# Step 1 of a fused convolution and gated-MLP kernel: other homes for six convolution taps, and four additions on another engine

## The chip, the cores and the metric

One core of a Trainium2 chip runs the whole program. The metric is the device time of one execution in microseconds (us), the median of several runs. The engines are TensorE (PE in the profile, with its weight loads PEld), VectorE (DVE), ScalarE (ACT), GpSimd (POOL) and SyncE (SP). SP and POOL also issue DMAs; a DMA that adds to its destination (an accumulation) is issued by POOL here.

## The reference, cut to what matters

```python
# x (8, 4096, 192), weight (8, 7): a causal depthwise convolution over the sequence, softmaxed taps per head
w = softmax(weight, axis=-1)
x_pad = np.concatenate([np.zeros((B, 6, D)), x], axis=1)
x_unf = x_pad[:, idx, :].reshape(B, S, K, H, group)      # idx: 7 shifted windows
x = np.einsum('hk,bskhg->bshg', w, x_unf).reshape(B * S, D)
# w_in (192, 2048), w_out (2048, 192)
h = x @ w_in
g = h * (1.0 / (1.0 + np.exp(-1.702 * h)))
return (g @ w_out).astype(np.float32)
```

## The kernel before

The 32768 tokens are worked in 32 steps ("big" in the code), each of 2 x 512 tokens. A step has a first half (`hidden`), which computes `x @ w_in` in fp32 by a scheme of fewer products over sums of operands, and the gelu, and a second half (`second`), which computes `g @ w_out` and stores. Step 0 has its own code. Each engine runs its instructions in the order in which the code issues them; the framework adds a wait on a semaphore where an instruction needs what another engine or a DMA has written, and also where it overwrites what another still has to read.

The order inside `hidden` is written out in the list `HIDDEN`. Its entries: `mm` is a product of TensorE (line 709) into one of four pairs of PSUM banks p0 to p3; `copy` and `join` move and combine banks (ScalarE or VectorE, lines 802, 804 and 817); `gelu i` is ScalarE's activation into rows of the buffer `g` (line 826 from PSUM in two halves, line 833 from SBUF in one instruction); `early` is a sum of rows of `g` on VectorE (lines 435 and 437); `over` makes the common sum of the next step (pair 12) by two additions and sends it across partitions with two DMAs of SP (line 609); `ve` makes further sums of the next step on GpSimd; `fetch` is the first product of the next step, which reads pair 12.

While step s runs, the convolution of a later step is made, in three blocks (0, 1, 2) of two column groups. A tap k of a block is one ScalarE instruction that multiplies the shifted input by the tap's weight, into a place of its own, its home (tap 0 goes to its final place in `conv_t`, "own"). The seven homes are then added in a tree: accumulation (i, j) adds home j to home i, in the order (1,2), (3,4), (5,6), (0,1), (3,5), (0,3). Homes are free places in larger buffers: `spot(i)` is one of the two pieces of `osbs` (0, 1), of three pieces of `room` (2 to 4), or, from 5 on, a block of `g`, and a home is a half of a spot (first index 0 or 2 of four).

Step 1 is special, because it makes step 2's convolution late. Blocks 0 and 2 of step 2 are tapped by ScalarE earlier (line 570) and added by DMA accumulations of GpSimd (line 600). The middle block, block 1, is tapped from the list `beside`: after the second `join` of step 1, each further join runs one entry, and entries 0 to 6 hold two weight sums of VectorE and tap j of the middle block (`middle_tap`, ScalarE, line 1096). Homes 1 to 6 are in the table `MIDDLE` as (spot, half), and `middle_tree` issues the block's accumulations (line 1108). The last two accumulations of block 2, (3,5) and (0,3), are left over in the list `tree` and issued by `end_taps` inside `middle_tap`, at tap 3 and tap 5, so they stand between the middle block's accumulations in GpSimd's queue; four accumulations for sums of w_out (line 482, "forms") stand ahead. `over` of step 1 runs at the third `turn`.

The rows of `g` that a spot covers are written by certain gelus. For the homes of this case: spots 11 and 12 at half 0 by gelu 5, spots 11 and 12 at half 2 by gelu 7, spot 14 at half 0 by gelu 8, spot 15 at half 0 by gelu 9, spot 17 at half 2 by gelu 14. The gelus stand in `HIDDEN` in the order 0, 6, 4, 1, 2, 5, 9, 3, 10, 11, 8, 7, 14, 12, 15, 13. Spot 14 at half 0 and spot 17 at half 2 hold pairs 17 and 18 of step 1, which early products of step 1 read.

Of the kernel before, what the change touches and what calls it, by code (L numbers as in the profile page):

```python
# [15 lines left out]
def kernel(  # L16
# [64 lines left out]
    vec, act = nc.vector, nc.scalar  # L81
# [56 lines left out]
    def spot(i):  # L138

        if i >= SPOTS:  # L140
            return block(*divmod(i - SPOTS, NG))
        flat = osbs[:, i * BLK : (i + 1) * BLK] if i < 2 else room[:, ROOMS[i - 2], :]
        return flat.rearrange("p (k t) -> p k t", k=NG)
# [47 lines left out]
    def pair(big, b):  # L191

        if b in SPOT_V:
            s, k = SPOT_V[b]
            return spot(s)[:, k : k + 2, :]
        o, x = places_of(big, b)
        return conv_t[:, o : x + 1 : x - o, :]

    def own(big):
        return conv_t[:, big % 2 * NR : big % 2 * NR + NR, :]  # L200
# [156 lines left out]
    for c in range(NC):  # L357
        part = sel[:, c, :].rearrange("i (h q) -> i h q", h=2)
        for sign in (1, -1):
            nc.gpsimd.affine_select(  # L360
                out=part,
# [71 lines left out]
    def add_up(v, dst, a, op, b, eng=vec):  # L433
        if op == "+":
            eng.tensor_add(v(dst), v(a), v(b))  # L435
        elif op == "-":
            eng.tensor_sub(v(dst), v(a), v(b))  # L437
        elif op == "n":
            vec.scalar_tensor_tensor(
                out=v(dst), in0=v(a), scalar=-1.0, in1=v(b), op0=ALU.mult, op1=ALU.subtract  # L440
            )
        else:
            vec.tensor_scalar_mul(v(dst), v(a), -1.0)
# [99 lines left out]
    def conv_src(big, c, k, ns=slice(0, 2)):  # L543
        return xts[big][:, c, ns, Q - PAD + k : Q - PAD + k + T]
# [43 lines left out]
    tree, to_add = [], {}  # L588
# [8 lines left out]
    def end_taps(left=0):  # L597
        while len(tree) > left:
            out, src = tree.pop(0)
            nc.gpsimd.dma_start(out=out, in_=src, accum_op=ALU.add)  # L600

    def sum_of(big, item, eng=None):

        add_up(lambda i: pair(big, i)[:, 0, :], *item, eng=eng or nc.gpsimd)
# [8 lines left out]
    def cross_run(big, b0, b1, eng=None):  # L613

        (o, x), n = places_of(big, b0), b1 - b0
        cross(conv_t[:, x : x + n, :], conv_t[:, o : o + n, :], eng)
# [158 lines left out]
    def hidden(big, tiles, work):  # L775
# [102 lines left out]

        def over():
            for item in SUMS_F:  # L880
                sum_of(big + 1, item)
            cross_run(big + 1, *FIRST)

        def when_more(f):
# [27 lines left out]
        def add(eng, what):  # L912
# [4 lines left out]
        do = dict(  # L917
            add=add, mm=mm, copy=copy, join=join, gelu=gelu, turn=turn, tap=tap, early=early, vl=vl, fetch=lambda: fetch(big + 1, tiles[NEXT[0]]) if more else None,
            over=when_more(over), ve=when_more(lambda i: sum_of(big + 1, SUMS_H[i])),
            vc=when_more(lambda b: cross_run(big + 1, b, b + 1)),  # L920
        )
# [7 lines left out]
    def second_first(between, fetch, last_taps):  # L929
# [152 lines left out]
        for j in range(max(K, (n - 2) // 2)):  # L1082
            def more(j=j):
                sums_w_in(FETCH[0], 3 + 2 * j, 5 + 2 * j)
                if j < K:
                    middle_tap(j)
            beside.append(more)

    after_copy, beside = [], []
    MIDDLE = ((11, 0), (12, 0), (3, 0), (15, 0), (11, 2), (3, 2))  # L1090

    def middle_tap(k):
        dst = own(2)[:, 2:4, :]
        s, h = MIDDLE[k - 1]
        home = spot(s)[:, h : h + 2, :] if k else dst
        act.mul(home, conv_src(2, 1, k), cw[:, 1, k : k + 1])
        end_taps({3: 1, 5: 0}.get(k, 2))
        middle_tree({2: 1, 4: 1, 6: 2}.get(k, 0))

    middle_pairs = [(1, 2), (3, 4), (5, 6), (0, 1), (3, 5), (0, 3)]  # L1100
# [1 line left out]
    def middle_tree(n):  # L1102
        for i, j in [middle_pairs.pop(0) for _ in range(n)]:
            out, src = (
                spot(MIDDLE[q - 1][0])[:, MIDDLE[q - 1][1] : MIDDLE[q - 1][1] + 2, :] if q else own(2)[:, 2:4, :]
                for q in (i, j)
            )
            nc.gpsimd.dma_start(out=out, in_=src, accum_op=ALU.add)
# [390 lines left out]
```

## Time and profile before

| | |
|---|---|
| median of 3 runs (lowest to highest) | 2274.39 us (2274.36 to 2275.14) |
| the profiled execution: its own time, its span | 2274.35 us, 2272.6 us |
| mean granted clock of TensorE | 0.997 |
| busy: PE, PEld, DVE, ACT, POOL | 99%, 59%, 93%, 75%, 43% of the span |
| GpSimd's DMA queue (accumulations): packets, MB | 67216, 169.05 |

The page of the profile gives sums over the whole span. The case is in a stretch of some 60 us near its start (about 97 to 183 us), so the views that count are those that can be cut to a window: the timeline (start, duration, engine, line, operation, destination <- source, shape, count, and in brackets how long the engine had been idle and what released it), the waits (who waited for what: total us, times, longest), the DMA issues (size, time from issue to landing) and the windows (busy time of PE, PEld, DVE, ACT, POOL with the count of instructions, then the granted clock, the DMA share and GB/s). Each row of the timeline may merge several equal instructions in sequence.

### The profile page before, as it was taken

The numbers are of one execution on the slowest core, as the hardware profiler recorded it, in microseconds if no ns is written. First come the engines' busy times: TensorE is split into PE (matmuls) and PEld (weight loads), VectorE is DVE, ScalarE is ACT, GpSimd is POOL, SyncE is SP. The second block draws the span as 40 slices with busy tenths as digits, with TensorE's granted clock in tenths as the row PEclk, the third lists the DMA queues.
The fourth block names the chain that finished last, engine by engine and source line by source line (L and its number), as shares of the span: only waits on it lengthen the run. The fifth ranks groups of instructions, "written<-read, shape, count | busy, mean of one in ns | idle before, by whom it ended". The sixth has DMA issues, their size and how long they took to land.

```text
span 2272.6 us, 63912 instructions
## 1 busy us (share of the span) xinstructions
PE 2249.9 (99%) x25090; PEld 1348.5 (59%) x25090; DVE 2108.6 (93%) x3261; ACT 1714.6 (75%) x3342; POOL 987.8 (43%) x1015
## 2 busy tenths in 40 slices
PE   9979999999999999999999999999999999999999
PEld 5445556666566665566665666655666656666554
DVE  8979999999999999999999999999999999999998
ACT  8857877777777778777777777787777777777854
POOL 1444543444543445434445434454344454344510
PEclk9989999999999999999999999999999999999999
DMA  9987788767787667787677876677876778765743
GB/s 205 178 153 145 140 154 167 142 138 143 143 165 155 138 138 142 154 161 147 138 146 141 165 154 138 138 142 152 164 146 138 145 140 166 155 137 112 138 97 71
DMA packets 342859, 331.24 MB, mean 146 GB/s; under 512 B 131744, under 2 KB 280864, under 8 KB 342560
## 3 DMA queue, kind: packets, MB, share of 16 engines
q0 software_dynamic: 67216, 169.05, 42.3%
q1 hardware_dynamic: 273696, 157.72, 30.3%
q8 instruction: 199, 3.26, 0.6%
q14 instruction: 100, 0.82, 0.1%
q10 hardware_dynamic: 1648, 0.39, 0.1%
HBM read 53.15 MB, written 25.17 MB: 34 GB/s over the span
## 4 chain that ended last, share of the span: by engine, by line
PE 92%; DVE 1%; DMA 0%; issue 0%; POOL 0%; DVEq 0%; POOLq 0%
PE slot L709 35%; PE slot L1199 28%; PE sums L1199 17%; PE sums L709 12%; DMA g<-g 0%; DVE g L437 0%; DVE room L437 0%; DVE osbs L437 0%; DVE g L435 0%; DVE room L435 0%; DVE osbs L1118 0%; POOL g L1175 0%; DVE g L817 0%; POOL room L595 0%; DVE osbs L435 0%
## 5 line engine op out<-in xcount | busy, mean ns | idle before, releaser
L709 PE MATMUL slot<-conv_t,w_in_s 64*128 64x512 f32 x3372 | 823.6, 593 | 13.8 <-ACT g L826 12.3
L1199 PE MATMUL slot<-g,w_form 128*32 128x256 f32 x5872 | 713.4, 379 | 0.0
L709 PEld LDWEIGHTS slot<-conv_t,w_in_s 64*128 64x128 f32 x3372 | 450.2, 187 | 299.0 <-issue 177.7
L437 DVE TENSOR_TENSOR g<-g 128x1024 f32<-128x1024 f32 x372 | 443.4, 1219 | 11.0 <-ACT g L833 3.8
L1199 PE MATMUL sums<-g,w_form 128*32 128x256 f32 x3800 | 422.0, 379 | 0.0
L1199 PEld LDWEIGHTS slot<-g,w_form 128*32 128x32 f32 x5872 | 363.7, 110 | 90.0
L826 ACT ACTIVATE g<-slot 128x512 f32<-128x512 f32 x494 | 265.1, 625 | 139.1 <-PE slot L709 126.5
L709 PE MATMUL sums<-conv_t,w_in_s 64*128 64x512 f32 x1284 | 346.1, 592 | 0.8 <-ACT osbs L802 0.5
L1199 PE MATMUL slot<-g,w_out_s 128*32 128x256 f32 x4080 | 321.3, 379 | 1.1 <-DVE room L435 1.1
L1175 POOL DMA_DIRECT2D g<-g x124 | 116.3, 938 | 453.8 <-PE slot L1199 290.7
L1224 ACT COPY room<-slot 32x256 f32<-32x256 f32 x434 | 158.5, 365 | 186.7 <-PE slot L1199 172.7
L570 ACT ACTIVATE g<-xt,cw 128x512 f32<-128x512 f32 x389 | 270.2, 719 | 4.4
L437 POOL TENSOR_TENSOR conv_t<-conv_t 128x256 f32<-128x256 f32 x210 | 193.2, 938 | 155.0 <-PE slot L709 93.0
L1199 PEld LDWEIGHTS sums<-g,w_form 128*32 128x32 f32 x3800 | 210.8, 110 | 69.7
L1199 PEld LDWEIGHTS slot<-g,w_out_s 128*32 128x32 f32 x4080 | 166.0, 110 | 127.4 <-ACT g L826 11.4
L915 POOL TENSOR_TENSOR conv_t<-conv_t,g 128x512 f32<-128x512 f32 x174 | 238.6, 1392 | 4.6
L709 PEld LDWEIGHTS sums<-conv_t,w_in_s 64*128 64x128 f32 x1284 | 171.2, 187 | 105.5 <-issue 56.2
L833 ACT ACTIVATE g<-g 128x1024 f32<-128x1024 f32 x155 | 170.6, 1101 | 0.0
L915 POOL TENSOR_TENSOR g<-g 128x512 f32<-128x512 f32 x87 | 110.7, 1272 | 122.4 <-ACT g L570 120.1
L1224 ACT COPY room<-sums 32x256 f32<-32x256 f32 x217 | 79.3, 365 | 103.9 <-PE sums L1199 91.1
L709 PE MATMUL slot<-g,w_in_s 64*128 64x512 f32 x556 | 147.8, 589 | 0.0
L826 ACT ACTIVATE g<-sums 128x512 f32<-128x512 f32 x188 | 103.7, 615 | 58.4 <-PE sums L709 57.7
(251 smaller groups left out, 3911.3 us busy)
## 6 DMA issues: line engine op xcount, KB each, us to landing
g<-g POOLq DMA_DIRECT2D x124, 512.0 KB, 6.6
conv_t<-conv_t SPq DMA_DIRECT2D x844, 64.0 KB, 2.0
xin<-in_x_dram SPq DMA_DIRECT2D x240, 180.0 KB, 6.3
out_dram<-osbs SPq DMA_DIRECT2D x186, 128.0 KB, 2.6
g<-g POOLq DMA_DIRECT2D x67, 256.0 KB, 6.6
g<-g SPq DMA_DIRECT2D x248, 64.0 KB, 3.6
g<-room POOLq DMA_DIRECT2D x31, 512.0 KB, 5.9
g<-osbs POOLq DMA_DIRECT2D x30, 512.0 KB, 6.6
```

The lines of the kernel that those rows point to most:

```text
L437: eng.tensor_sub(v(dst), v(a), v(b))
L570: act.mul(home, conv_src(big, c, k), cw[:, c, k : k + 1])
L709: nc.tensor.matmul(slot[h], w_in_s[halves[h], a, v * P : (v + 1) * P], src, start=first, stop=True, skip_group_check=True,)
L826: act.activation(dst[:, :, h, :], ot(bank(src, h)), AF.Gelu_apprx_sigmoid, scale=float(sign))
L833: act.activation(dst.rearrange("p o h t -> p h o t"), src, AF.Gelu_apprx_sigmoid, scale=float(sign))
L915: (vec if eng == "v" else nc.gpsimd).tensor_add(dst, dst, home)
L1175: nc.gpsimd.dma_start(out=spot(dst), in_=spot(a), accum_op=ALU.add)
L1199: nc.tensor.matmul(dst, w, t, start=first, stop=last, skip_group_check=True)
L1224: act.copy(to, d)
```

## The change

Three things change, all of them in step 1 only. The six homes of the middle block's taps are others. The accumulations (3,5) and (0,3) of block 2, issued before as DMAs by GpSimd at taps 3 and 5, become additions of VectorE (128 x 512 each) at taps 5 and 6. The two additions of the common sum of step 2 (128 x 256 each) go from GpSimd to VectorE.

```diff
         def over():
             for item in SUMS_F:
-                sum_of(big + 1, item)
+                sum_of(big + 1, item, vec if big == 1 else None)
             cross_run(big + 1, *FIRST)
...
-    MIDDLE = ((11, 0), (12, 0), (3, 0), (15, 0), (11, 2), (3, 2))
+    MIDDLE = ((14, 0), (11, 2), (3, 0), (17, 2), (3, 2), (11, 2))
 
     def middle_tap(k):
         dst = own(2)[:, 2:4, :]
         s, h = MIDDLE[k - 1]
         home = spot(s)[:, h : h + 2, :] if k else dst
         act.mul(home, conv_src(2, 1, k), cw[:, 1, k : k + 1])
-        end_taps({3: 1, 5: 0}.get(k, 2))
+        if k in (5, 6):
+            out, src = tree.pop(0)
+            vec.tensor_add(out, out, src)
+            assert len(tree) == 6 - k
         middle_tree({2: 1, 4: 1, 6: 2}.get(k, 0))
```

Homes 2 and 6 are now one place, spot 11 at half 2. On GpSimd the order of the middle block's accumulations stays, without the two of block 2 and the two additions between them. On VectorE the first new addition stands ahead of a join of two banks and the second ahead of the early sum that follows gelu 2; the common sum stands ahead of a transposition of the input of step 3. TensorE's and SP's order stays.

## Prediction

> **What bounds the kernel now.** I read the page's first line, the waits of TensorE over the whole span, and then the timelines of each engine around the one long wait.
>
> ```profile
> span 2272.6 us, 63912 instructions
> ```
>
> ```profile
> PE slot L709 <- ACT g L826: 12.3, 1, 12.3
> PE sums L500 <- POOL osbs masks.py:199: 1.4, 1, 1.4
> PE slot L1199 <- DVE room L435: 1.1, 1, 1.1
> ```
>
> The profiled execution took 2274.35 us, a span of 2272.6 and 1.75 around it; the median of the runs shown is 2274.39, so 0.04 lies between them. TensorE waits in only three places for over 1 us, and one holds most of it: 12.3 us for a gelu (L826). Its place, on TensorE:
>
> ```profile
> 120.16 1.08 PE L709 MATMUL sums<-conv_t,w_in_s 64*128 64x512 f32 x3
> 133.57 6.53 PE L709 MATMUL slot<-conv_t,w_in_s 64*128 64x512 f32 x20 [12.33 <-ACT g L826]
> ```
>
> This is step 1's first product, from 121.24 to 133.57. ScalarE's timeline tells why:
>
> ```profile
> 117.27 1.07 ACT L802 COPY osbs<-slot 128x512 f32<-128x512 f32 x2 [1.16 <-DMA out_dram<-osbs]
> 118.23 0.73 ACT L1096 ACTIVATE room<-xt,cw 128x512 f32<-128x512 f32 x1
> 118.86 1.05 ACT L833 ACTIVATE g<-g 128x1024 f32<-128x1024 f32 x1
> 131.94 2.06 ACT L826 ACTIVATE g<-slot 128x512 f32<-128x512 f32 x4 [12.03 <-DMA conv_t<-g]
> ```
>
> The four rows are the copy ahead of it, tap 6 of the middle block (L1096), gelu 2 (L833), and gelus 5 and 9 in two halves each. Gelu 5 writes spots 11 and 12 at half 0, the homes of taps 1 and 2, and waits for a DMA into conv_t that reads g. GpSimd's timeline and the time to landing of single issues show which:
>
> ```profile
> 106.65 2.97 POOL L600 DMA_DIRECT2D g<-g  x3
> ...
> 116.01 2.59 POOL L1108 DMA_DIRECT2D g<-g  x1
> ...
> 126.67 1.55 POOL L1108 DMA_DIRECT2D conv_t<-g  x1
> 129.06 0.72 POOL L435 TENSOR_TENSOR conv_t<-conv_t 128x256 f32<-128x256 f32 x1 [0.85 <-issue]
> ...
> 138.63 4.40 POOL L437 TENSOR_TENSOR conv_t<-conv_t 128x256 f32<-128x256 f32 x5 [2.60 <-PE slot L709]
> ```
>
> ```profile
> g<-g POOLq DMA_DIRECT2D x1, 256.0 KB, 9.3
> ...
> g<-g POOLq DMA_DIRECT2D x1, 256.0 KB, 8.0
> ...
> conv_t<-g POOLq DMA_DIRECT2D x1, 256.0 KB, 5.2
> ```
>
> The last landing row is the issue at 126.67, accumulation (0,1) of the middle block: it lands at 131.87 and gelu 5 starts at 131.94. The second is the issue at 116.01, accumulation (1,2), which lands at 124.0. The first is the last of the three issued from 106.65 on, accumulation (5,6) of block 2: issued near 107.7 (a third of the way each), landed near 117.0. So the stall is a write that waits for a late reader, and (0,1) is late because it stands in GpSimd's queue behind two accumulations of block 2.
>
> **The change part by part.**
>
> *Homes.* Gelu 5 no longer writes any middle tap's home: homes 1, 2, 4 and 6 go to spots that gelus 8, 7 and 14 write, all later in the list. The 12-us wait goes. What is late next is on the same engine, two instructions earlier: tap 6 now shares its home (spot 11, half 2) with tap 2, so it may not be written before accumulation (1,2) has read tap 2. That accumulation is issued behind the same instructions as before, four form additions, and its inputs are ready; I keep its landing at 124.0. Queued behind tap 6 on ScalarE are gelus 2, 5 and 9, and TensorE waits for gelu 9. With the 0.07 us that the semaphore took above, tap 6 starts at 124.1; tap to gelu 2 is 0.63 (118.86 less 118.23), gelu 2 is 1.05, so gelu 5 starts at 125.8. TensorE followed gelu 5's start by 1.63 (133.57 less 131.94), so it restarts at 127.4: a stall of 6.2 instead of 12.3. **TensorE gains 6.2 us.** The other new homes cost nothing: tap 1's and tap 4's places are last read by products that precede the taps in the list and on TensorE by microseconds, and gelus 8, 7 and 14 stand far behind gelu 9 in the list, more products ahead of them than the accumulations that read their places take. Uncovered, each would cost the rest of an accumulation, at most the 9.3 above.
>
> *The two accumulations of block 2, and the common sum.* VectorE's timeline and its grouped rows price them:
>
> ```profile
> 119.94 1.23 DVE L437 TENSOR_TENSOR g<-g 128x1024 f32<-128x1024 f32 x1 [2.46 <-ACT g L833]
> ...
> 124.20 0.29 DVE L437 TENSOR_TENSOR w_in_s<-w_in_s 128x128 f32<-128x128 f32 x1
> 135.56 1.30 DVE L817 TENSOR_TENSOR sums<-room,osbs 128x512 f32<-128x512 f32 x2 [11.06 <-ACT g L826]
> ...
> 138.57 1.82 DVE L817 TENSOR_TENSOR slot<-g,osbs 128x512 f32<-128x512 f32 x2
> ...
> 141.81 1.30 DVE L817 TENSOR_TENSOR slot<-slot,room 128x512 f32<-128x512 f32 x2 [0.73 <-PE slot L709]
> ...
> 143.70 1.18 DVE L437 TENSOR_TENSOR room<-g,osbs 128x1024 f32<-128x1024 f32 x1
> ```
>
> ```profile
> L437 DVE TENSOR_TENSOR conv_t<-conv_t 128x256 f32<-128x256 f32 x2 | 0.7, 397 | 0.0
> ```
>
> Two additions of 128x512 cost VectorE 0.65 each (half of 1.30). The first waits for (5,6) of block 2, so for 117.0; a join with the weights' sums queues behind it and ends about 118.9. The product that needs that join runs up to 121.24, before the stall, so nothing of this reaches the end. Its cover is 0.8 us plus the stall.
>
> What does reach it: in the stall before, VectorE worked ahead. The early sum waits for gelu 2, which now ends at 125.8 instead of 119.9, and from its start to the end of the row at 124.20 there are 4.55 us of work (124.49 less 119.94). So VectorE is free for the join of 135.56 at 130.35, where the gelu that releases that join, moved by 6.2, allows 129.36: 1.0 late. The common sum of the fetched product, two sums for 0.7, lies behind it: 1.7 late. Two things give time back: the 0.73 us for which VectorE waited for TensorE at 141.81, and 0.5 us at 138.57, where the same two-half join took 1.82 instead of 1.30 while GpSimd ran its five sums. These five meet another VectorE instruction now: the three accumulations ahead of them start after tap 6, at 124.8, so they end about 2 us sooner than before and the sums start near 136.5, under the early sum of 143.70, moved to about 138. Each of the five took 0.88 (4.40 through five) instead of 0.72. I put 0 to 1.0 for the meeting, and take 0.4, near the 0.5 of the row. VectorE is then 1.7 - 0.73 - 0.5 + 0.4 = 0.9 late against TensorE's shift.
>
> The Trainium skill's page "SBUF — State Buffer", section "Who interferes with whom", speaks against the moved sums here: a VectorE instruction with two SBUF inputs shuts out a GpSimd instruction that reads SBUF for its whole length. By it the early sum, 1.18 long, could wait 0.7 more; the row at 138.57 agrees with 0.5, and the sum by the rule alone would be 0.3 us longer.
>
> Does VectorE's lateness count? The chain that ended last answers:
>
> ```profile
> 146.69 0.60 DVE g L817
> ...
> 182.45 1.93 PE slot L1199 x32
> ```
>
> From 146.69 to 182.45 it runs by VectorE and the DMAs that it feeds, and at 182.45 TensorE had waited 1.1 for it (third row of the waits). So VectorE's shift is what the rest inherits; TensorE has 1.1 us to spare. After 182.45 no wait over 1 us is left, and the rest only moves.
>
> On SyncE the crossing DMAs of the common sum wait for VectorE instead of GpSimd; the sum ends near 132.3 now and near 130.6 before, and the fetched product stands eleven products behind TensorE's restart, of which the first five took 6.5 (the row at 133.57), so it comes after 138. The two crossings have 6 us; uncovered, they cost what they take beyond that. GpSimd loses two issues and two sums, which nobody waits for.
>
> *Sum.* 2274.35 - 6.2 + 0.9 = **2269.0 us**.
>
> **The clock.** The stall costs TensorE more than its length:
>
> ```profile
> 123.00:125.00 2.00, 0.00 (x0) 0.00 (x0) 1.46 (x4) 0.00 (x0) 0.00 (x0) 0.61 1.10 189
> ...
> 137.00:138.00 1.00, 1.00 (x7) 0.88 (x6) 1.00 (x2) 0.68 (x2) 0.00 (x0) 0.96 1.06 182
> ```
>
> The granted clock (third column from the end) averages 0.61 over 123 to 125 and 0.96 over 137 to 138: it fell to one half some 2.2 us into the stall (at 123.4) and came back at 137.1, 3.5 us after the restart. A stall of 6.2 us is still longer than 2.2, so the half clock comes again, and my sum keeps these 3.5 us.
>
> **The rivals.** (a) *The half clock lasts longer.* If the return at 137.1 is not 3.5 us behind the restart by nature but by luck, it may take up to twice as long. Then TensorE loses half of up to 3.5, 1.7 us; VectorE waits for TensorE again at the join of 141.81, and the 0.9 shrinks to about 0.4: 2274.35 - 6.2 + 1.7 + 0.4 = 2270.3. The one stall here can't say. The Trainium skill's page "TensorE: Matmul & The Clock Gate", section "What's actually happening", has the gate decide at the ends of free-running windows of about 3.4 us; fall and return here are 13.7 apart, four such windows, so the trace agrees, and by the rule a restart 0.5 us into a window brings the clock back after 3 us or after 6.3. (b) *VectorE becomes the bound.* If neither the 0.73 nor the 0.5 comes back and the meeting costs its full 1.0, VectorE is 2.7 late: 2270.9. (c) *The stall goes almost altogether*, if (1,2) lands as soon after its issue as (0,1) did, 5.2 instead of 8.0: 2.8 us more, 2266.2. Against it: the queue ahead of it is unchanged. (d) *The change doesn't do what it says*: another reader of gelu 5's or 9's places is as late as the old one; the time stays at 2274. I find none in the order of the code. (e) *Slower*: tap 6's wait stands ahead of gelus 2, 5 and 9, and each us by which (1,2) lands later moves TensorE by one. With 0.9 lost to VectorE the gain is gone when it lands 5.3 us later, at 129.3, 13.3 after its issue, and 0.2% is lost at 133.9, 17.9 after it: 2279. The longest of the three rows is 9.3.
>
> **How the numbers follow.** Forecast 0.55 (2268 to 2269.8), (a) 0.18, (b) 0.10, (c) 0.07, (d) 0.06, (e) 0.04. About 0.2%, 4.5 us, is what a measurement can tell from no change, so faster means below 2269.8: the forecast 0.55, a quarter of (a), (c), together 0.67, and some of (b), 0.70 in all. Within 0.2%: the rest of (a) and (b), and (d), 0.26. Slower: (e), 0.04. The range 2266.2 to 2271.5 holds the forecast, (a), (b), and the edge of (c).
>
> **What would show it.** Right: tap 6 idle before it for 5 to 6 us, released by the DMA g<-g issued near 116 and landing near 124; TensorE's long wait 5.5 to 6.5; the half clock once more, at a shorter stretch; VectorE with no long idle between 126 and 141; the five GpSimd sums near 136. Wrong: a long wait at gelu 5 or 9 itself, a landing of (1,2) away from 124 by over 1 us, or TensorE waiting at 182 by much more than 1.1.

## The result, and the profile after

The changed kernel takes 2270.39 us (median of 21 runs, 2269.47 to 2272.0), the kernel before in the same comparison 2275.14 (21 runs, 2273.35 to 2276.65): ratio 0.998, 95% interval 0.9973 to 0.9986, a gain of 4.75 us. The forecast was 2269.0 against 2274.35, a gain of 5.35, with a range of 2266.2 to 2271.5. The profiled execution of the changed kernel took 2269.52 us, 4.83 less than that of before (2274.35); they lie 0.87 and 0.79 under the two medians, so the rows below explain the difference rather than the medians themselves.

The page's first line and the waits of TensorE over the span, changed kernel (total us, times, longest):

```profile
span 2267.8 us, 63911 instructions
```

```profile
PE slot L709 <- ACT g L826: 6.1, 1, 6.1
...
PE slot L1202 <- DVE room L435: 0.3, 1, 0.3
```

The long wait is still for a gelu, at half its length, and the wait of 1.1 us late in step 1 has shrunk to 0.3 (it is L1202 now, because the edit moved the lines below it). TensorE's timeline at the stall:

```profile
119.82 1.08 PE L709 MATMUL sums<-conv_t,w_in_s 64*128 64x512 f32 x3
127.04 6.32 PE L709 MATMUL slot<-conv_t,w_in_s 64*128 64x512 f32 x20 [6.14 <-ACT g L826]
```

The stall runs from 120.90 to 127.04. ScalarE shows that it is now tap 6 (L1096) that waits, ahead of gelu 2 (L833) and of gelus 5 and 9 (L826), and for another DMA, g<-g:

```profile
123.86 0.72 ACT L1096 ACTIVATE g<-xt,cw 128x512 f32<-128x512 f32 x1 [5.85 <-DMA g<-g]
124.49 1.04 ACT L833 ACTIVATE g<-g 128x1024 f32<-128x1024 f32 x1
125.43 2.04 ACT L826 ACTIVATE g<-slot 128x512 f32<-128x512 f32 x4
```

GpSimd's timeline, and the landing of its issue at 115.58 (KB, us to landing):

```profile
115.58 2.58 POOL L1111 DMA_DIRECT2D g<-g  x1
...
136.34 5.35 POOL L437 TENSOR_TENSOR conv_t<-conv_t 128x256 f32<-128x256 f32 x5 [2.97 <-DMA conv_t<-room]
```

```profile
g<-g POOLq DMA_DIRECT2D x1, 256.0 KB, 8.2
```

115.58 and 8.2 make 123.78: accumulation (1,2) lands there, and 0.08 later tap 6 overwrites tap 2. The five sums run from 136.34 to 141.69. VectorE's timeline shows what they meet:

```profile
116.34 0.69 DVE L1099 TENSOR_TENSOR g<-g 128x512 f32<-128x512 f32 x1 [1.75 <-DMA g<-g]
...
118.68 0.68 DVE L1099 TENSOR_TENSOR conv_t<-conv_t,g 128x512 f32<-128x512 f32 x1
125.56 1.23 DVE L437 TENSOR_TENSOR g<-g 128x1024 f32<-128x1024 f32 x1 [6.20 <-ACT g L833]
...
130.02 1.29 DVE L817 TENSOR_TENSOR sums<-room,osbs 128x512 f32<-128x512 f32 x2
131.23 0.42 DVE L435 TENSOR_TENSOR conv_t<-conv_t 128x256 f32<-128x256 f32 x1
131.68 0.42 DVE L437 TENSOR_TENSOR conv_t<-conv_t 128x256 f32<-128x256 f32 x1
...
133.86 1.29 DVE L817 TENSOR_TENSOR slot<-g,osbs 128x512 f32<-128x512 f32 x2
...
135.75 1.26 DVE L817 TENSOR_TENSOR slot<-slot,room 128x512 f32<-128x512 f32 x2
...
137.61 1.23 DVE L437 TENSOR_TENSOR room<-g,osbs 128x1024 f32<-128x1024 f32 x1
138.76 2.35 DVE L817 TENSOR_TENSOR sums<-g,room 128x512 f32<-128x512 f32 x2
...
142.22 1.21 DVE L437 TENSOR_TENSOR osbs<-g 128x1024 f32<-128x1024 f32 x1
```

The kernel before has these two last instructions as

```profile
144.81 1.29 DVE L817 TENSOR_TENSOR sums<-g,room 128x512 f32<-128x512 f32 x2
...
147.20 1.22 DVE L437 TENSOR_TENSOR osbs<-g 128x1024 f32<-128x1024 f32 x1
```

So the join of two halves at 138.76 takes 2.35 instead of 1.29. What the first half of the step gains and loses: TensorE restarts 6.53 us sooner (133.57 less 127.04; 0.34 of it lay ahead of the stall already, 120.16 less 119.82, and the stall itself is 12.33 less 6.14, 6.19, shorter). The last sum above starts 4.98 sooner (147.20 less 142.22): VectorE is 6.53 less 4.98, 1.55, late.

What lies behind step 1's first half, from the chain that ended last (start, duration), first before and then after:

```profile
166.77 10.85 DMA g<-g
...
182.45 1.93 PE slot L1199 x32
```

```profile
161.72 10.21 DMA g<-g
...
176.76 1.93 PE slot L1202 x32
```

The first row of each pair is an accumulation of GpSimd in the step's second half. It starts 5.05 sooner and takes 0.64 less, so at 176.76 TensorE is 5.69 ahead. In step 6 some 0.9 of it is lost again. Four products of an operand in g, before and after:

```profile
491.39 1.16 PE L709 MATMUL slot<-g,w_in_s 64*128 64x512 f32 x4
```

```profile
485.82 1.73 PE L709 MATMUL slot<-g,w_in_s 64*128 64x512 f32 x4
```

They take 0.57 longer. The second half of step 6 starts at 497.74 before and at 492.97 after, 4.77 sooner, and from there to the end the two traces stay 4.8 apart. 5.69 less 0.9 is the 4.8 by which the spans differ. VectorE and GpSimd show what is different ahead of these products, before and after:

```profile
486.32 1.82 DVE L817 TENSOR_TENSOR slot<-room,osbs 128x512 f32<-128x512 f32 x2
...
486.62 2.10 POOL L437 TENSOR_TENSOR conv_t<-conv_t 128x256 f32<-128x256 f32 x2 [0.98 <-PE slot L709]
```

```profile
480.98 2.40 DVE L817 TENSOR_TENSOR slot<-room,osbs 128x512 f32<-128x512 f32 x2
...
480.95 1.86 POOL L437 TENSOR_TENSOR conv_t<-conv_t 128x256 f32<-128x256 f32 x2 [0.99 <-PE slot L709]
```

It is a second meeting of VectorE and GpSimd. Before, GpSimd's two sums start 0.30 behind VectorE's join, and the join takes 1.82; after, they start 0.03 ahead of it, and it takes 2.40. Against the shift of 5.69 VectorE enters this join 0.35 late and leaves it 0.93 late, which is the loss. Why it enters late stays open.

### The profile page after: what moved, and what is told of

It is laid out like the page before. It is cut to its first block, busy times and chain, and to the rows that moved or that the text cites. A ratio compares the mean times of both kernels' runs of the same rounds, so it can differ in the third digit from the quotient of the medians.

```text
span 2267.8 us, 63911 instructions
## 1 busy us (share of the span) xinstructions
PE 2252.2 (99%) x25090; PEld 1360.1 (60%) x25090; DVE 2111.8 (93%) x3265; ACT 1716.0 (76%) x3342; POOL 985.5 (43%) x1011
## 4 chain that ended last, share of the span: by engine, by line
PE 93%; DMA 3%; DVE 2%; issue 1%; ACT 1%; POOL 0%; POOLq 0%; DVEq 0%; ACTq 0%
PE slot L709 35%; PE slot L1202 28%; PE sums L1202 17%; PE sums L709 12%; DMA g<-g 2%; DMA w_form<-w_form 1%; DMA w_form<-w_out_s 0%; DMA osbs<-in_moe_w_out_dram 0%; PE slot L1290 0%; DVE slot L817 0%; DVE g L437 0%; POOL conv_t L600 0%; DVE xt L518 0%; DVE conv_t L553 0%; DVE room L437 0%
## 5 line engine op out<-in xcount | busy, mean ns | idle before, releaser
L1202 PE MATMUL slot<-g,w_form 128*32 128x256 f32 x5872 | 713.4, 379 | 0.0
L709 PEld LDWEIGHTS slot<-conv_t,w_in_s 64*128 64x128 f32 x3372 | 458.8, 187 | 284.2 <-issue 173.1
L1202 PE MATMUL sums<-g,w_form 128*32 128x256 f32 x3800 | 422.0, 379 | 0.0
L1202 PEld LDWEIGHTS slot<-g,w_form 128*32 128x32 f32 x5872 | 363.7, 110 | 90.0
L826 ACT ACTIVATE g<-slot 128x512 f32<-128x512 f32 x494 | 265.4, 624 | 127.2 <-PE slot L709 126.8
L1202 PE MATMUL slot<-g,w_out_s 128*32 128x256 f32 x4080 | 321.3, 379 | 0.5 <-DVE room L435 0.3
L1202 PEld LDWEIGHTS sums<-g,w_form 128*32 128x32 f32 x3800 | 210.8, 110 | 69.7
L1202 PEld LDWEIGHTS slot<-g,w_out_s 128*32 128x32 f32 x4080 | 166.0, 110 | 126.7 <-ACT g L826 11.4
L833 ACT ACTIVATE g<-g 128x1024 f32<-128x1024 f32 x155 | 170.5, 1100 | 0.0
L915 POOL TENSOR_TENSOR g<-g 128x512 f32<-128x512 f32 x87 | 110.9, 1274 | 121.9 <-ACT g L570 119.7
L826 ACT ACTIVATE g<-sums 128x512 f32<-128x512 f32 x188 | 103.9, 615 | 59.6 <-PE sums L709 58.8
```

The costliest lines, as they stand in the source:

```text
L709: nc.tensor.matmul(slot[h], w_in_s[halves[h], a, v * P : (v + 1) * P], src, start=first, stop=True, skip_group_check=True,)
L826: act.activation(dst[:, :, h, :], ot(bank(src, h)), AF.Gelu_apprx_sigmoid, scale=float(sign))
L833: act.activation(dst.rearrange("p o h t -> p h o t"), src, AF.Gelu_apprx_sigmoid, scale=float(sign))
L915: (vec if eng == "v" else nc.gpsimd).tensor_add(dst, dst, home)
L1202: nc.tensor.matmul(dst, w, t, start=first, stop=last, skip_group_check=True)
```

## The experiments

Three theories stood at the start. T1: the gain is tap 6's new wait in place of gelu 5's, and nothing but the homes makes it. T2: the moves to VectorE give part of it, since (0,1) would otherwise stand behind two accumulations. T3: what the forecast missed by is the meeting of the five GpSimd sums with VectorE. Each gain below is against the kernel before in the same comparison (medians 2274.58, 2274.65 and 2274.71 in the three comparisons). Edits are shown against the changed kernel unless the text says otherwise.

**The homes alone** (homes_only).

```diff
 MIDDLE = ((14, 0), (11, 2), (3, 0), (17, 2), (3, 2), (11, 2))
-        if k in (5, 6):
-            out, src = tree.pop(0)
-            vec.tensor_add(out, out, src)
-            assert len(tree) == 6 - k
+        end_taps({3: 1, 5: 0}.get(k, 2))
-                sum_of(big + 1, item, vec if big == 1 else None)
+                sum_of(big + 1, item)
```

> The new homes alone; the two accumulations of block 2 and the common sum are GpSimd's again. My theory (the stall that is left is tap 6's wait for the reader of the place it shares with tap 2, accumulation (1,2), which lands at 123.8): the stall stays at 6.1 us, since (1,2) stands where it stood; VectorE is 0.8 us freer (the common sum took 131.23 to 132.05 in the changed kernel), GpSimd's five sums come some 2 us later and meet other additions. About 2269.5 to 2270.5, within 1 us of the changed kernel. Rival (the shorter queue of GpSimd is what shortened the stall): the stall is over 9 us and the time above 2273.

2269.31 us, ratio 0.9978 (0.9968 to 0.9987), gain 5.27, 0.2 under what was expected. TensorE's longest wait, then two joins of VectorE and the five sums of GpSimd:

```profile
PE slot L709 <- ACT g L826: 6.3, 1, 6.3
```

```profile
138.75 2.35 DVE L817 TENSOR_TENSOR sums<-g,room 128x512 f32<-128x512 f32 x2
141.02 1.27 DVE L817 TENSOR_TENSOR g<-room,slot 128x512 f32<-128x512 f32 x2
...
138.62 5.42 POOL L437 TENSOR_TENSOR conv_t<-conv_t 128x256 f32<-128x256 f32 x5 [2.51 <-DMA conv_t<-room]
```

The stall is that of the full change, and so is the stretched join. The homes make the whole gain; the moves add nothing to it that the intervals could tell, and the meeting doesn't come from them. The second join, of which one operand (slot) lies in PSUM, takes its usual 1.27 although the five sums run beside it, from 138.62 to 144.04; the first, with both operands in SBUF, is stretched.

**The moves alone** (moves_only).

```diff
-    MIDDLE = ((14, 0), (11, 2), (3, 0), (17, 2), (3, 2), (11, 2))
+    MIDDLE = ((11, 0), (12, 0), (3, 0), (15, 0), (11, 2), (3, 2))
```

> The old homes, with the additions on VectorE. My theory: gelu 5 waits for accumulation (0,1) again. (0,1) no longer stands behind block 2's accumulations but still needs (1,2), landed at 123.8; it lands some 4.3 us later (125.41 to 129.70 in the changed kernel), near 128.2, so the stall is about 9 us and the time about 2271.5 to 2272.5. Rival (the shorter queue does it all): stall 6 us, 2270. Rival (the moves bring nothing): stall 12, 2275.

2272.13 us, ratio 0.999 (0.9982 to 0.9999), gain 2.45. Waits of TensorE, and of ScalarE from 100 to 150:

```profile
PE slot L709 <- ACT g L826: 9.0, 1, 9.0
```

```profile
ACT g L826 <- DMA conv_t<-g: 8.7, 1, 8.7
```

With the old homes gelu 5 waits for (0,1) as before, which lands 3.3 us sooner because two accumulations no longer stand ahead of it. So the moves are worth something as long as (0,1) is the binding wait: T2 holds there, and the two parts don't add up (5.27 and 2.45 alone, 4.75 together).

**Tap 6 with a home of its own** (tap6_home).

```diff
-    MIDDLE = ((14, 0), (11, 2), (3, 0), (17, 2), (3, 2), (11, 2))
+    MIDDLE = ((14, 0), (11, 2), (3, 0), (17, 2), (3, 2), (16, 2))
```

> The changed kernel with one more home moved: tap 6 goes to spot 16, half 2, whose last reader (accumulation (3,4) of block 2) landed at 114.5, and whose next writer is gelu 11. My theory: tap 6 starts at 117.9 without a wait, TensorE's stall falls from 6.1 to below 0.7, the clock stays up, TensorE is some 7 us earlier (5.9 of stall, 1.5 of half clock); VectorE, which then has no slack, gives back 0 to 2.5: 2263 to 2266. Rival (another reader is as late as (1,2)): the stall moves to gelu 5, 9 or 11 and the time stays within 1.5 us of 2270.4.

2265.65 us, ratio 0.9962 (0.9948 to 0.9975), gain 8.93. Its longest wait of TensorE is another one:

```profile
PE slot L1202 <- DVE g L437: 1.7, 2, 0.9
```

No wait for a gelu over 0.2 is left and the clock stays at 1.0. The shared home of taps 2 and 6 was the last long stall of the stretch, and without it VectorE is what TensorE waits for most. The five sums and VectorE's three groups beside them:

```profile
136.18 8.05 POOL L437 TENSOR_TENSOR conv_t<-conv_t 128x256 f32<-128x256 f32 x5 [3.64 <-DMA conv_t<-room]
```

```profile
136.85 1.75 DVE L435 TENSOR_TENSOR g<-g,osbs 128x1024 f32<-128x1024 f32 x1
138.53 1.76 DVE L437 TENSOR_TENSOR osbs<-osbs,g 128x1024 f32<-128x1024 f32 x1
140.21 7.49 DVE L437 TENSOR_TENSOR g<-g 128x1024 f32<-128x1024 f32 x5
```

**The accumulation's landing** (forms_later): the four DMAs for sums of w_out, which stand ahead of (1,2) in GpSimd's queue, go behind it. ScalarE's copies for these sums move with them.

```diff
-            elif len(seen) == 1:
+            elif len(seen) == 2:
                 add_forms(3)
```

> The changed kernel with the four additions for w_out's sums (and ScalarE's copies for them) one turn later, so that accumulation (1,2) stands right behind block 2's (0,1) in GpSimd's queue. My theory (tap 6 waits for (1,2), whose landing is set by what is queued ahead): (1,2) lands near 119.4 instead of 123.8, the stall is about 2 us, 2264.5 to 2267. Rival ((1,2) takes its 8 us whatever is ahead): it is issued near 113.4 and lands near 121.5, stall about 4 us, 2267.5 to 2269.

2265.02 us, ratio 0.9959 (0.9947 to 0.9972), gain 9.56. TensorE's wait, GpSimd's issue and its landing:

```profile
PE slot L709 <- ACT g L826: 1.5, 1, 1.5
```

```profile
114.30 1.13 POOL L1111 DMA_DIRECT2D g<-g  x1
```

```profile
g<-g POOLq DMA_DIRECT2D x1, 256.0 KB, 5.7
```

(1,2) lands at 120.0 instead of 123.78, and tap 6 starts at 120.02: 1.28 of that because (1,2) is issued sooner, 2.5 because it takes 5.7 to land instead of 8.2 with less ahead of it. The landing that the prediction took as given was set by the queue, and the stall followed it.

**Without the five sums** (no_five): their `ve` entries in step 1 are left out, so that step 2 lacks these sums and the run tells of the time alone.

```diff
-            ve=when_more(lambda i: sum_of(big + 1, SUMS_H[i])),
+            ve=when_more(lambda i: sum_of(big + 1, SUMS_H[i]) if big > 1 else None),
```

> The changed kernel without GpSimd's five sums of step 2 in step 1 (they are left out). My theory: these sums, which met the two halves of the join that feeds step 1's last products (138.76 to 141.11 in the changed kernel, 1.22 each instead of 0.69), are what made VectorE later than I had summed: each half falls back to 0.69, TensorE starts the second half 1.0 to 1.3 us sooner after its restart (16.9 us in the changed kernel), 2269 to 2269.6. Rival (the additions moved to VectorE are what it lost): the halves stay at 1.22 or the time stays at 2270.4.

2269.18 us, ratio 0.9977 (0.9968 to 0.9987), gain 5.47. VectorE:

```profile
140.01 1.29 DVE L817 TENSOR_TENSOR sums<-g,room 128x512 f32<-128x512 f32 x2
```

The join is back at 1.29, so the five sums were what stretched it (T3). From its restart to the second half TensorE takes 16.14 (127.99 to 144.13) instead of 16.90 (127.04 to 143.94): 0.76 less where 1.0 to 1.3 had been expected, in a profile in which the half clock lasted 5.4 us after the restart, against 3.1. The gain is 0.7 above that of the changed kernel, less than the intervals are wide.

**Own home, all moves undone** (tap6_all_back): the edits of homes_only on tap6_home, and shown against it.

```diff
 MIDDLE = ((14, 0), (11, 2), (3, 0), (17, 2), (3, 2), (16, 2))
-        if k in (5, 6):
-            out, src = tree.pop(0)
-            vec.tensor_add(out, out, src)
-            assert len(tree) == 6 - k
+        end_taps({3: 1, 5: 0}.get(k, 2))
-                sum_of(big + 1, item, vec if big == 1 else None)
+                sum_of(big + 1, item)
```

> The homes of tap6_home, with both accumulations of block 2 and the common sum on GpSimd again. My theory: with tap 6's wait gone, the middle block's later accumulations become the late readers: (5,6) stands behind (0,3) of block 2, which waits for (3,5) to land near 125.5, so (5,6) lands near 130.5 and (0,1) near 132 instead of 127.4 and 129.1, and gelus 11 and 8, which overwrite their places and ran at 128 to 129.5, wait some 2.5 us: 2267.5 to 2269.5, against 2265.7 with the moves. Rival (the moves are worth nothing, the homes do it all, as homes_only had it): within 0.7 us of 2265.7.

2269.73 us, ratio 0.9979 (0.997 to 0.9988), gain 4.92; its 11 runs spread from 2267.89 to 2273.26, and the median is 0.2 above what was expected. ScalarE waits, and the chain has the same stretch of TensorE later than in tap6_home (second fence):

```profile
ACT g L826 <- DMA room<-g: 2.5, 1, 2.5
```

```profile
176.51 1.93 PE slot L1199 x32
```

```profile
172.87 1.93 PE slot L1202 x32
```

Here the moves are worth 3.6 us at that point, 2.9 between the two profiled spans (the loss of step 6 is in that of tap6_home alone) and 4.0 in the medians. ScalarE's wait for (5,6) is only a part of it: one and the same sum of VectorE starts at 159.27 here and at 158.27 in tap6_home, 1.0 apart. Another 2.0 arises in the second half, where VectorE waits 3.1 for an accumulation osbs<-room of GpSimd and 1.2 in tap6_home. So GpSimd's queue binds in both places and taking two accumulations out of it pays, but how they bring about the later wait is not shown.

**Own home, five sums left out or moved** (tap6_no_five, tap6_ve_vec). The first leaves the `ve` entries of step 1 out, with the edit of no_five; the second gives them to VectorE at the end of the first half, with their crossings behind. Shown is the second's edit against tap6_home.

```diff
-            ve=when_more(lambda i: sum_of(big + 1, SUMS_H[i])),
+            ve=when_more(lambda i: sum_of(big + 1, SUMS_H[i], vec if big == 1 else None)),
-                    held.clear()
-                    while waiting:
-                        waiting.pop(0)()
...
         for item in HIDDEN:
             do[item[0]](*item[1:])
+        held.clear()
+        while waiting:
+            waiting.pop(0)()
```

> tap6_home without GpSimd's five sums (left out). There each of them took 1.72 us and alternated with VectorE's sums of 128x1024, and TensorE waited 0.9, 0.8 and 0.7 us for VectorE behind them. If the two engines shut each other out for whole instructions, VectorE gets back 2 to 2.6 us and most of it reaches the end: 2263 to 2264. If VectorE's own work is the bound: within 0.7 us of 2265.7.

> tap6_home with the five sums on VectorE at the end of the first half, where the last accumulation has landed, and their crossing DMAs behind them. Five sums of 0.33 us are 1.65 on VectorE's path instead of the 2 to 2.6 that the meeting costs: 2264.5 to 2265.5 if the meeting is priced right. If the meeting costs nothing: 2267.3.

2263.83 us, ratio 0.9954 (0.9941 to 0.9966), gain 10.82; and 2264.4 us, ratio 0.9957 (0.9944 to 0.9969), gain 10.25, 0.1 under its expectation. The chains, in this order:

```profile
170.94 1.93 PE slot L1202 x32
```

```profile
172.50 1.93 PE slot L1202 x32
```

Leaving the sums out brings 1.93 by the chain (172.87 less 170.94) and 1.8 by the medians. Moving them brings only 0.37 in step 1, because VectorE now does their work itself; the medians differ by 1.25. The other 0.9 is the loss in step 6, as far as the two profiles go: that of tap6_home has it and that of tap6_ve_vec has not. tap6_ve_vec is a full version and beats both kernels of the case; forms_later, above, is as quick within the intervals.

**The common sum back on GpSimd** (sum_back), the rest as in the changed kernel.

```diff
-                sum_of(big + 1, item, vec if big == 1 else None)
+                sum_of(big + 1, item)
```

> The changed kernel with only the common sum on GpSimd again. It took VectorE from 131.23 to 132.10 in the changed kernel. My theory (it delays VectorE by 0.8, of which TensorE's own pace hides some 0.4, since the next join then waits for TensorE again; the five sums still meet the later join): 2269.7 to 2270.4, not told from the changed kernel by the time, and the trace shows an idle of VectorE of some 0.3 us before the join that follows the second transposition. Rival (the common sum on GpSimd comes late and the fetched product waits for its crossing): slower than the changed kernel by over 0.5.

2269.47 us, ratio 0.9976 (0.9966 to 0.9985), gain 5.24, 0.2 under the expectation and like homes_only. As expected VectorE then waits for TensorE ahead of the join that follows the second transposition (0.49 at 137.52, some 0.3 expected). Whether the common sum's move costs the changed kernel anything is not shown: the gains differ by some 0.5 (5.24 against 4.75), less than the intervals are wide. The profiled run, at 2270.56 the longest of its ten, shows something else. Windows (us, busy time of PE, PEld, DVE, ACT, POOL, then granted clock, DMA share, GB/s):

```profile
133.00:134.00 1.00, 1.00 (x5) 0.81 (x3) 1.00 (x3) 1.00 (x4) 0.00 (x0) 0.50 0.24 63
134.00:135.00 1.00, 1.00 (x6) 0.82 (x5) 1.00 (x2) 1.00 (x4) 0.83 (x1) 0.79 0.00 0
```

TensorE restarted at 127.95 and the clock came back at 134.4, 6.5 us later. In the changed kernel it had been 3.1:

```profile
124.00:130.00 6.00, 2.96 (x7) 2.56 (x9) 4.41 (x9) 6.00 (x11) 2.59 (x3) 0.50 0.55 93
130.00:131.00 1.00, 1.00 (x6) 0.83 (x5) 1.00 (x3) 0.86 (x2) 0.00 (x0) 0.94 1.00 174
```

**Both cures together** (tap6_ve_forms): tap6_ve_vec with the edit of forms_later.

> tap6_ve_vec with the four additions for w_out's sums one turn later, as in forms_later: is there more to get by joining the two cures? My theory: no stall is left that the earlier landing of (1,2) could shorten, so what is left is the half us by which ScalarE's copies for these sums held TensorE back before the stall: 2263.5 to 2264.5. Rival (the queue still matters): 2262 or less.

2265.74 us, ratio 0.996 (0.9945 to 0.9974), gain 8.97: a miss, no better than either alone. Its TensorE has a wait that is 0.3 in tap6_ve_vec:

```profile
PE sums L709 <- ACT osbs L802: 2.0, 1, 2.0
```

This wait, for a copy that waits for an output store, lies near 111, and the half clock shows from 112.9 to 119.7. Neither explains the miss. The profile of sum_back has the same wait (1.9), with the four DMAs in their old place. And three of the five runs of tap6_ve_forms have a mean granted clock of 1.0, where 6.8 us at half clock would cost 0.0015 of it, and take 2265.05, 2265.58 and 2266.39. Why the two cures don't add up stays open.

## Why the prediction was right, point by point

*Homes, right.* Tap 6 waits for (1,2): landing 123.78 (124.0 forecast), tap 6 at 123.86 (124.1), stall 6.14 (6.2). tap6_home and forms_later show both ends of the reason: take the shared home away and the stall is gone, bring the landing forward and the stall shrinks to 1.5.

*The additions of block 2, right.* 0.69 and 0.68 (0.65), and no cost: with them in place and only the common sum back (sum_back) the gain is that of the homes alone.

*VectorE's lost head start, right.* The join came at 130.02 (130.35); against 135.56 less TensorE's shift of 6.53 that is 1.0 late. The common sum took 0.82 (0.7). Both refunds came: no idle time is left before the join of 135.75, and the join of 133.86 takes 1.29 instead of 1.82. At 135.75 VectorE is 0.47 late (141.81 less 6.53 is 135.28), which is 1.7 less 0.73 less 0.5.

*The meeting with the five sums, the term that was mis-sized.* Forecast 0.4 at the early sum, bounds 0 to 1.0; measured 1.06, and at the instruction behind it. The early sum of 137.61 was hardly touched (1.23 against 1.18); both halves of the join at 138.76 were. So VectorE came out 1.55 late and not 0.9. The Trainium skill's page "SBUF — State Buffer", section "Who interferes with whom", has an instruction of VectorE with two SBUF inputs and one of GpSimd that reads SBUF exclude each other for whole instructions; 2.35 instead of 1.29 for the join and 5.35 instead of 4.40 for the five sums agree with it. The sum by that rule, 0.3 us longer, was the nearer one. The mistake was to carry a price measured at one meeting (0.5) to another without asking how many instructions of each side would meet.

*The end of the step, right, and its remainder.* VectorE's lateness set the start of the second half, as forecast: TensorE begins it at 143.94 instead of 148.98, 5.04 sooner, so 1.49 of its 6.53 is gone there, and its 1.1 of slack late in the step was used up to 0.3. Three small terms were not in the sum: 0.34 gained ahead of the stall, 0.64 gained at an accumulation and 0.9 lost in step 6. 6.53 - 1.55 + 0.64 - 0.9 gives 4.72, where the spans differ by 4.8. That the total came so near is in part luck: TensorE's larger shift (0.33) and the accumulation (0.64) made up for 0.97 of the 1.55 that the meeting (0.65) and step 6 (0.9) took beyond the forecast.

*The loss in step 6 is the same kind of meeting.* The five profiles that have it (changed kernel, tap6_home, forms_later, no_five, tap6_no_five) show the join of 480.98 at 2.36 to 2.40 and the four products at 1.72 or 1.73; the seven others show 1.82 or 1.83 and 1.16 to 1.20. The forecast stopped at step 1 with "the rest only moves". What puts GpSimd ahead of VectorE there in just these five is not shown.

*The rivals.* (a), a longer half clock, did not happen in the changed kernel's profile (3.1 us after the restart) but did in two others with nearly the same stall (5.4 in no_five, 6.5 in sum_back). It was no case against the forecast but a spread between runs of TensorE's lost time, up to (6.5 - 3.1) / 2 = 1.7 us, and the range rightly held it. (b) came halfway: the meeting cost its full upper bound, but both refunds were paid. (c) to (e) did not happen.

## What to carry to other kernels

When a write waits for a late reader, look at the next write in the same engine's queue too: here the new homes ended a wait of 12 us and left one of 6 us, in the one home that two taps shared, and one more changed number, (16, 2), gained another 4 us. Taking work out of a queue paid here only while a landing of that queue was the wait that binds: the same moves brought 2.45 us with the old homes, nothing with the new ones and 4 us with tap 6's own home. And where sums of VectorE and GpSimd come to run beside each other, count the instructions of both sides that will meet, in the later steps too, and price each by most of an instruction of the other side: here 0.53 for one of VectorE that met sums of 0.72. In step 6 a join was held up by 0.6 more in the five profiles in which GpSimd's sums came earlier against it, by 0.03 us ahead of it in the changed kernel instead of 0.30 behind it.

## What had not been expected of the hardware

The half clock's end is not a fixed time behind the restart. It lasted 3.5 us before, 3.1 in the changed kernel and 6.5 in sum_back. From fall to return it was 13.7 us before (123.4 to 137.1), 6.8 after (123.3 to 130.1) and 10.2 in sum_back (124.2 to 134.4): four, two and three times 3.4 us, on a grid that stands elsewhere in each run. The Trainium skill's page "TensorE: Matmul & The Clock Gate", section "What's actually happening", has free-running windows of about that length, and these three spans agree. The other profiles with a long stall fit as well: 6.8 in homes_only and no_five, 10.2 in moves_only. Reckoned back from the returns in steps of 3.41, the changed kernel restarted (127.04) 0.33 us into a window and had the clock back at its end, at 130.12; sum_back restarted (127.95) 0.37 us into one and had it back only at the end of the next, at 134.41.

VectorE and GpSimd slow each other when their sums run beside each other: a VectorE sum of 128x1024 went from 1.22 to 1.75, and five GpSimd sums, 0.72 each alone, from 4.40 to 8.05 (tap6_home). That is some 0.5 for each instruction of VectorE and 0.9 for each of GpSimd, about three quarters of an instruction of the other side. A join with one operand in PSUM was not slowed (1.27 in homes_only).
